# Two PSUM banks as two tiles instead of one, in the attention bursts of a fused attention and feed-forward kernel

## The chip, the cores and the metric

The kernel runs on one core of one Trainium2 chip. The metric is the device time of one execution in microseconds (us), median over runs. A core has TensorE (PE, whose weight loads the profile lists as PEld), VectorE (DVE), ScalarE (ACT), GpSimd (POOL) and SyncE (SP, which issues the DMAs). Each engine runs its own list of instructions in order and waits for other engines through semaphores.

## The reference

Linear attention with decay, in blocks of 64 tokens, then a feed-forward layer with a squared ReLU. All in float32. Per batch (4) and head (8), with sequence 768 and head size 64:

```
for each block of 64 tokens:
    intra = ((q @ k.T) * Dmask) @ v          # Dmask[i,j] = lam**(i-j) for i >= j, else 0
    inter = (q * lam**(i+1)) @ kv_state
    out   = intra + inter
    kv_state = lam**64 * kv_state + (k * lam**(63-j)).T @ v
x = out as 3072 tokens x 512
h = x @ w_in                                  # 512 -> 2048
y = (max(h, 0) ** 2) @ w_out                  # 2048 -> 512
```

## The kernel before, in words

**Units of work.** Tokens go in chunks of 128 (two blocks of 64), numbered t = 0 to 23, six to a batch. Four chunks make a slice m of 512 tokens, the width of one feed-forward step; there are six slices. The 2048 hidden features go in 16 groups f of 128. Float32 products of the feed-forward layer are made of three products of a high and a low part (wh, wl for weights, xh, xl or gh, gl for data).

**Stages.** The opening does the attention of chunks 0 to 3. Then come two plain slices (m = 0 and 1, the constant PLAIN): for each f, `hidden` (L574) makes h by 12 matmuls, ACT and DVE square it and split it into gh and gl (`positive`, `square`, `rest`), and `project` (L605) adds the product of the group before into four accumulators `acc`. In m = 0 the attention of chunks 4 to 7 is spread over the f loop (`look`, `attend`). In m = 1, the "slice 2" of the change's title, each of f = 0 to 8 holds one **burst** (L430) for chunk t = 8 + f. After that two pairs of slices are done by a seven-product scheme (`pair`, L760, 8 calls to a pair of slices); in the first pair of slices each call holds a burst for chunks 17 to 24, the last of which has no chunk ahead.

**A burst** is attention work of TensorE alone, in matmuls of 64 by 64 by 64 that run on the four quarters of the array, all recorded at line 384. Its three parts, in the order of the code:

- `scores(t)`: k by q of chunk t, 16 matmuls (each is two records in the trace, 32 in all). Those with operands on partitions 0 to 63 (row 0) write the half `hi_` of bank y (a tile named h from the pool ps_h), those on partitions 64 to 127 (row 1) the half `lo_` of bank x[1].
- `result(t - 1)`: masked scores by v, and q by the state, of the chunk before: 32 matmuls (64 records); row 0 writes the other half of y, row 1 the half `lo_` of x[0].
- `news(t)`: k by v of chunk t, which feeds the state: up to 16 matmuls (32 records); row 1 writes the half `hi_` of x[0], row 0 the half `hi_` of x[1].

x[0] and x[1] are the two banks of one tile `att` from the pool ps_a, which holds one such tile at a time. So bank x[1] is written first by row 1 (scores) and later by row 0 (news). Between the two stands the **mark**: a copy of one element on ACT (L439) that reads the last score in x[1]. It stands on ACT behind what the argument `meanwhile` issues: in slice 2 that is `positive(h)` (L588), in a pair it is `positive(c21)` and `square_high(c21)`. Nothing reads the marked value; the copy is there for the waits it makes.

**What sets the order.** Each engine's order is the order of the code. The framework puts in the waits: an instruction that writes a tile waits for earlier readers and writers of that tile on other engines. The first matmul of `result` that writes att waits for the mark, since both touch att.

**After a burst** ACT copies the result out of y and x[0] (`keep`, L447), DVE reads the scores (`masked`, L463, two reads) and the news (`state`, L483, first from x[0], then from x[1]), POOL scales q of the next chunk (`prep_q`, L452) and k (`prep_k`), ACT makes copies with the partition halves swapped (`copy_vx` L162, `copy_qx` L167), and SP issues loads for later chunks (`load_v` L151, `load_kq` L145 and L132). In f = 2, 3, 4, 6, 7 and 8 (and later in 10 and 12) of slice 2, `w_parts` (L662) also writes sums of weights to memory, which the pairs fetch again.

**PSUM** has eight banks: ps_h two, ps_a two (one `att` tile), and four for ps_o in the opening, which are given back and taken by the accumulators ps_acc.

Of the kernel before, what the change touches and what calls it, by code (L numbers as in the profile page):

```python
# [7 lines left out]
F32 = mybir.dt.float32  # L8
# [5 lines left out]
PSUM = bass.MemoryType.PSUM  # L14

P = 128
# [6 lines left out]
DM = H * D  # L23
# [19 lines left out]
def body(ctx: ExitStack, tc: tile.TileContext, qT, kT, kvq, lam, w, out):  # L43
# [3 lines left out]
    wk = ctx.enter_context(tc.tile_pool(name="wk", bufs=2))  # L47
    small = ctx.enter_context(tc.tile_pool(name="small", bufs=1))
    ps_h = ctx.enter_context(tc.tile_pool(name="ps_h", bufs=2, space=PSUM))
    ps_a = ctx.enter_context(tc.tile_pool(name="ps_a", bufs=1, space=PSUM))  # L50
    opening = ExitStack()
    ps_o = opening.enter_context(tc.tile_pool(name="ps_o", bufs=2, space=PSUM))
    V = nc.vector
    rows = [slice(j * D, (j + 1) * D) for j in range(2)]
# [18 lines left out]
    def two_banks(pool, name):  # L73
        return pool.tile([P, 2, DM], F32, name=name)
# [62 lines left out]
    def load(t):  # L137
        place(t)
        load_all(t)
        load_kf(t)  # L140
# [9 lines left out]
    def load_v(t):  # L150
        nc.sync.dma_start(out=chunk[t]["v_flat"], in_=kvq[t, :, DM : 2 * DM])  # L151

    def load_vx(t):
        for y, r in enumerate(rows):
            nc.sync.dma_start(
                out=chunk[t]["vx"][r].rearrange("p a j d -> p (a j d)"),
                in_=kvq[t, rows[1 - y], DM + 2 * y * C : DM + 2 * (y + 1) * C],
            )
# [115 lines left out]
    x = ZP  # L274
# [12 lines left out]
    for k in range(4):  # L287
# [10 lines left out]
        lambda o, x, y, op=op: V.tensor_tensor(out=o, in0=x, in1=y, op=op)  # L298
# [4 lines left out]
    lo_, hi_ = s[:, 0 : NS - 1], s[:, 1:NS]  # L303
# [16 lines left out]
    for k in range(NS - 1):  # L320
        n = 1 << k
        x = (tr if k else s)[:, k : k + 1]
# [67 lines left out]
    def of(x):  # L390
        return [x[:, k] for k in range(2)]

    def scores(t, banks, begun=(), keys=range(2)):
        g = Group(banks, begun, keys)
        sc_of[t] = [x[:, 0 : NPR * L] for x in banks]
        k_, q_ = chunk[t]["kf"], chunk[t]["q"]
        for b in range(2):
            for a in range(2):
                for y in range(2):
                    for j, r in enumerate(rows):  # L400
                        p = 2 * y + a
                        g.put(
                            j, y, (2 * b + a) * L,
                            k_[r, p, (1 - b) * L : (2 - b) * L], q_[r, p, b * L : (b + 1) * L],
                        )
        return g.begun

    def news(t, banks, at, begun=(), keys=range(2)):
        g = Group(banks, begun, keys)
        k_, v_ = chunk[t]["k"], chunk[t]["v"]  # L410
        n = 2 if t % NCB < NCB - 1 else 1
        u_of[t] = [banks[1 - b][:, at : at + NPR * D] for b in range(n)]
        for a in range(2):
            for j in range(2):
                for y in range(2):
                    for b in range(n):
                        r, p = rows[1 - b], 2 * y + a
                        g.put(1 - b, y, at + (2 * a + j) * D, k_[r, p, j], v_[r, p, j])
        return g.begun
# [8 lines left out]


    def burst(t, done, ahead, meanwhile):  # L430
        x = of(two_banks(ps_a, "att"))
        y = ps_h.tile([P, DM], F32, name="h")
        lo_, hi_ = slice(0, NPR * L), slice(NPR * L, DM)
        begun = set()
        if ahead:
            begun = scores(t, [y[:, hi_], x[1][:, lo_]], begun, "ec")
        meanwhile()
        if ahead:
            nc.scalar.copy(mark[:, 2:3], sc_of[t][1][D : D + 1, NPR * L - 1 : NPR * L])  # L439
        o = [y[:, lo_], x[0][:, lo_]]  # L440
        if done:
            begun = result(t - 1, o, begun, "ea")
        if ahead:
            news(t, [x[1][:, hi_], x[0][:, hi_]], 0, begun, "ca")
        return o

    def keep(t, o):  # L447
# [126 lines left out]
    def hidden(m, f, xh, xl):  # L574
        h = ps_h.tile([P, N], F32, name="h")
        for _ in range({1: 10, 2: 6}.get(f, 0) if m == 0 else 0):
            nc.tensor.matmul(h, wh[:, 0, 0:P], xh[:, 0], start=True, stop=True)
        k = 0
        for wt, x in ((wh, xh), (wl, xh), (wh, xl)):
            for kt in range(KT):  # L580
                nc.tensor.matmul(  # L581
                    h, wt[:, w_in(f), kt * P : (kt + 1) * P], x[:, kt], start=k == 0, stop=k == 11
                )
                k += 1
        return h

    def positive(h):
        nc.scalar.activation(h, h, AF.Relu)  # L588
# [207 lines left out]
    def new_x(m):  # L796
        xs_of[m] = [wk.tile([P, KT, N], F32R, name=n, tag=n) for n in ("xh", "xl")]
# [96 lines left out]
    for m in range(PLAIN):  # L894
        if m == 0:
            new_x(1)
        else:
            held += [
                wk.tile([P, KT, N], F32, name=f"held{k}", tag=n) for k, n in enumerate(("xh", "xl"))
            ]  # L900
        for f in range(NF):
            h = hidden(m, f, *xs_of[m])
            if m == 0:
                t = G + f // 4
                step = f % 4
                u_ = f + 2
                if step == 2:
                    o = two_banks(ps_a, "att")
                    result(t, of(o))
                    if t + 1 < 2 * G:  # L910
                        load(t + 1)
                        load_vx(t + 1)
                    else:
                        for n in (t + 1, t + 2):
                            load_kq(n)
                            load_v(n)
                if step == 1:
                    masked(t)
                    advance(t, 0)
                if u_ < NLOT:  # L920
                    if f:
                        clamp(u_)
                    if f == 1:
                        upper(u_ - 1)
                        lower(u_ - 1)
                    if f:
                        shift(u_)
                    sign(u_)
                if f > 1:
                    upper(u_ - 1)  # L930
                    lower(u_ - 1)
                if f:
                    turn(u_ - 1)
                if step == 1:
                    fade(t, 1)
                    advance(t, 1)
                if f == 0:
                    positive(h)
                    gh = square(h)
                    rest(m, f, h, gh)  # L940
                if u_ < NLOT:
                    rounded(u_)
                    wload(u_ + 3)
                if step == 0 and f:
                    prep_q(t)
                if step == 3 and t + 1 < 2 * G:
                    prep_k(t + 1)
                if f:
                    positive(h)
                    gh = square(h)  # L950
                    rest(m, f, h, gh)
                if step == 1:
                    copy_qx(t)
                if step == 2:
                    attend(t, o)
                if u_ + 1 < NLOT:
                    first(u_ + 1)
                if prev is not None:
                    project(*prev)
                if step == 0:  # L960
                    look(t)
                    fade(t, 0)
            else:
                t = 2 * G + f
                if f == 0:
                    prep_k(t)
                if f <= 2 * G:
                    x = burst(t, f > 0, True, lambda: positive(h))
                    rest(m, f, h, square(h))
                else:  # L970
                    squared(m, f, h)
                if 1 <= f <= 2 * G:
                    keep(t - 1, x)
                if f <= 2 * G:
                    masked(t)
                    state(t)
                    if f:
                        load_v(t + 1)
                    prep_q(t)
                    if t + 2 < SOLO:  # L980
                        load_kq(t + 2)
                    prep_k(t + 1)
                    copy_vx(t)
                if f - 1 in SUMS:
                    w_parts(SUMS.index(f - 1), S)
                if f in SUMS:
                    S = w_sums(SUMS.index(f))
                if f <= 2 * G:
                    copy_qx(t)
                if f == 2 * G + 1:  # L990
                    fetch(0)
                    fetch(1)
                if f > 2 * G:
                    x_sums(f - 2 * G - 1)
                    x_parts(f - 2 * G - 1)
                project(*prev)
            prev = (m, f)
# [6 lines left out]
    for d in range((NM - PLAIN) // 2):  # L1004
        m1, m2 = PLAIN + 2 * d, PLAIN + 2 * d + 1
        last = d == (NM - PLAIN) // 2 - 1
        for i in range(NPAIR):
            t = (PLAIN + 2) * G + i
# [93 lines left out]
```

## Time and profile before

| | |
|---|---|
| median of 3 runs | 596.24 us (596.09 to 596.43) |
| profiled execution | 595.19 us; its span, first to last instruction, 593.4 us, so 1.79 us lie around it |
| mean granted clock of TensorE | 0.997 |
| busy: PE, PEld | 578.0 us (97%), 471.8 us (80%) |
| busy: DVE, ACT, POOL | 320.4 us (54%), 316.7 us (53%), 70.9 us (12%) |
| chain that ended last | PE 88%, DVE 5%, ACT 5%, issue 1%, DMA 1% |
| DMA | 93.62 MB, mean 158 GB/s |

Times in the views are microseconds from the start of the span. A PE record is a matmul with a modelled end: matmuls overlap, so what counts as time on PE is the distance between starts, and the idle time that a view names before a record is shorter than the hole between the starts. In the timeline, equal instructions close together are merged into one row with their count, and a bracket gives the idle time before the row and what ended it.

### The profile page before, as it was taken

The page shows a single profiled execution, that of the slowest core. Times are in us where ns is not written, and L with a number is a line of the kernel's source. Part 1 is how long each engine was busy: PE and PEld are TensorE (multiplying, and loading weights), DVE is VectorE, ACT ScalarE, POOL GpSimd, SP SyncE. Part 2 cuts the span into 40 slices and gives each one's busy share as a digit, 9 for nine tenths or more (in the row PEclk, how much of TensorE's full clock was granted, in tenths as well). Part 3 has the DMA queues.
Part 4 walks back from the last instruction along what each step waited for, and adds up shares of the span by engine and source line. Part 5 has one row for each costly group of instructions (what it writes and reads, how often), then busy time and mean ns, then how long its engine had stood idle before and what let it go on. Part 6 is the DMA issues. An engine that isn't in the chain of part 4 may idle for free.

```text
span 593.4 us, 12762 instructions
## 1 busy us (share of the span) xinstructions
PE 578.0 (97%) x5240; PEld 471.8 (80%) x5240; DVE 320.4 (54%) x586; ACT 316.7 (53%) x579; POOL 70.9 (12%) x87
## 2 busy tenths in 40 slices
PE   8799999999999999999999999999999999999997
PEld 5677788787787888888888788888888888888885
DVE  7889999946867676534443333356433333334222
ACT  4598888945666555455454455543444444444221
POOL 7302221221323100011101010000000000000000
PEclk9999999999999999999999999999999999999999
DMA  8658567146897942855555554300264444421001
GB/s 333 223 203 276 176 233 264 38 144 196 276 363 234 357 151 98 273 172 180 161 143 159 176 163 118 132 1 0 58 192 125 122 124 120 122 62 72 1 0 71
DMA packets 51273, 93.62 MB, mean 158 GB/s; under 512 B 4624, under 2 KB 19472, under 8 KB 51216
## 3 DMA queue, kind: packets, MB, share of 16 engines
q1 hardware_dynamic: 51216, 92.82, 48.5%
q8 instruction: 41, 0.67, 0.5%
q14 instruction: 16, 0.13, 0.1%
HBM read 71.83 MB, written 20.97 MB: 156 GB/s over the span
## 4 chain that ended last, share of the span: by engine, by line
PE 88%; DVE 5%; ACT 5%; issue 1%; DMA 1%; POOL 0%; ACTq 0%; DVEq 0%; POOLq 0%
PE h L723 24%; PE acc L617 15%; PE acc L622 14%; PE acc L618 14%; PE h L581 12%; PE att L384 5%; PE h L384 2%; PE att L79 1%; DVE temp L298 1%; DVE A L232 1%; ACT gh L592 1%; ACT temp L588 1%; DMA raw<-in_w 1%; PE open L384 1%; DVE A L238 1%
## 5 line engine op out<-in xcount | busy, mean ns | idle before, releaser
L617 PE MATMUL acc<-wh,gh 128*128 128x512 f32 x384 | 151.9, 396 | 0.0
L618 PE MATMUL acc<-wl,gh 128*128 128x512 f32 x384 | 149.5, 389 | 0.0
L622 PE MATMUL acc<-wh,gl 128*128 128x512 f32 x384 | 149.4, 390 | 0.0
L617 PEld LDWEIGHTS acc<-wh,gh 128*128 128x128 f32 x384 | 72.0, 188 | 15.6
L622 PEld LDWEIGHTS acc<-wh,gl 128*128 128x128 f32 x384 | 72.1, 188 | 15.4
L618 PEld LDWEIGHTS acc<-wl,gh 128*128 128x128 f32 x384 | 72.1, 188 | 14.5
L602 DVE TENSOR_TENSOR gl<-h,gh 128x512 fp32r<-128x512 f32 x48 | 33.1, 689 | 74.2 <-ACT h L597 74.2
L588 ACT ACTIVATE h<-h 128x512 f32<-128x512 f32 x48 | 27.9, 582 | 74.0 <-PE h L581 40.3
L298 DVE TENSOR_TENSOR temp<-h,temp 128x512 f32<-128x512 f32 x48 | 33.0, 688 | 60.5 <-PE h L723 49.4
L723 PE MATMUL h<-wh,ring 128*128 128x512 f32 x224 | 60.0, 390 | 0.0
L588 ACT ACTIVATE temp<-temp 128x512 f32<-128x512 f32 x16 | 10.1, 632 | 88.6 <-DVE temp L298 88.6
L723 PEld LDWEIGHTS h<-wh,ring 128*128 128x128 f32 x224 | 42.0, 188 | 8.9 <-DVE r L298 0.3
L456 POOL TENSOR_TENSOR qs<-set,qpow 128x512 f32<-128x512 f32 (+1 forms) x21 | 24.9, 1187 | 179.2 <-PE att L384 160.9
L581 PE MATMUL h<-xh,wl 128*128 128x512 f32 x128 | 34.9, 394 | 1.6 <-DVE wl L247 1.5
L581 PE MATMUL h<-xh,wh 128*128 128x512 f32 x128 | 34.8, 394 | 1.1 <-ACT xh L562 0.7
L298 DVE TENSOR_TENSOR r<-h,temp 128x512 f32<-128x512 f32 x24 | 16.6, 692 | 34.1 <-PE h L723 33.0
L723 PE MATMUL h<-wl,ring 128*128 128x512 f32 x112 | 34.5, 389 | 0.0
L602 DVE TENSOR_TENSOR gl<-r,gh 128x512 fp32r<-128x512 f32 x24 | 16.6, 690 | 32.9 <-ACT gh L755 32.9
L581 PE MATMUL h<-xl,wh 128*128 128x512 f32 x128 | 34.2, 389 | 0.0
L755 ACT CAST gh<-r 128x512 fp32r<-128x512 f32 x24 | 14.9, 621 | 30.0 <-PE acc L618 30.0
L581 PEld LDWEIGHTS h<-xh,wl 128*128 128x128 f32 x128 | 23.6, 188 | 8.5 <-DVE wl L247 3.7
L723 PE MATMUL h<-wh 128*128 128x512 f32 x112 | 30.1, 390 | 0.0
(165 smaller groups left out, 1026.0 us busy)
## 6 DMA issues: line engine op xcount, KB each, us to landing
ring<-wd SPq DMA_DIRECT2D x56, 256.0 KB, 2.8
raw<-in_w SPq DMA_DIRECT2D x22, 512.0 KB, 5.5
set<-in_kvq SPq DMA_DIRECT2D x16, 512.0 KB, 4.2
wd<-hl SPq DMA_DIRECT2D x16, 512.0 KB, 5.8
wh<-wd SPq DMA_DIRECT2D x28, 256.0 KB, 2.8
wl<-wd SPq DMA_DIRECT2D x28, 256.0 KB, 2.9
set<-in_kT SPq DMA_DIRECT2D x22, 256.0 KB, 4.7
set<-in_w SPq DMA_DIRECT2D x10, 512.0 KB, 5.0
```

The source lines that it names most:

```text
L79: nc.tensor.matmul(w_[:, 0], st[:, 0, 0].rearrange("p a b -> p (a b)"), st[:, 0:2].rearrange("p n c a b -> p (n c a b)"), start=True, stop ...
L298: lambda o, x, y, op=op: V.tensor_tensor(out=o, in0=x, in1=y, op=op)
L384: nc.tensor.matmul(self.banks[row][rows[col], at : at + D], lhsT, rhs, start=key not in self.begun, stop=stop, skip_group_check=True,)
L456: nc.gpsimd.tensor_tensor(out=z, in0=x, in1=w_, op=ALU.mult)
L581: nc.tensor.matmul(h, wt[:, w_in(f), kt * P : (kt + 1) * P], x[:, kt], start=k == 0, stop=k == 11)
L588: nc.scalar.activation(h, h, AF.Relu)
L602: V.tensor_tensor(out=gl, in0=r, in1=gh.bitcast(F32), op=ALU.subtract)
L617: nc.tensor.matmul(accs[m][i], gh[:, cs], wh[:, j], start=f == 0, stop=False)
L618: nc.tensor.matmul(accs[m][i], gh[:, cs], wl[:, j], start=False, stop=False)
L622: nc.tensor.matmul(accs[m][i], gl[:, cs], wh[:, j], start=False, stop=end)
L723: nc.tensor.matmul(bank, w[:, kw * HALF + kt * P : kw * HALF + (kt + 1) * P], x_slot(2 * c + kt, kx), start=first and q == 0, stop=q == 5, ...
L755: nc.scalar.copy(gh, r_of[f])
```

## The change

`burst` takes two one-bank tiles b0 and b1 from a new pool ps_b in place of one two-bank tile. The pool ps_a, now placed at the right end of PSUM, is given back before m = 1, and ps_b is opened in its place. The first burst (f = 0 of m = 1), which has no result to make, no longer issues the mark, and its news of row 0 go to the half `lo_` of bank y, where row 0 has written its scores, instead of x[1]. Everything else of the kernel is as before.

```diff
     ps_h = ctx.enter_context(tc.tile_pool(name="ps_h", bufs=2, space=PSUM))
-    ps_a = ctx.enter_context(tc.tile_pool(name="ps_a", bufs=1, space=PSUM))
-    opening = ExitStack()
+    opening, middle = ExitStack(), ExitStack()
+    ps_a = middle.enter_context(tc.tile_pool(name="ps_a", bufs=1, side="right", space=PSUM))
     ps_o = opening.enter_context(tc.tile_pool(name="ps_o", bufs=2, space=PSUM))
...
     def burst(t, done, ahead, meanwhile):
-        x = of(two_banks(ps_a, "att"))
+        x = [ps_b.tile([P, DM], F32, name=f"b{k}") for k in range(2)]
         y = ps_h.tile([P, DM], F32, name="h")
         lo_, hi_ = slice(0, NPR * L), slice(NPR * L, DM)
         begun = set()
         if ahead:
             begun = scores(t, [y[:, hi_], x[1][:, lo_]], begun, "ec")
         meanwhile()
-        if ahead:
+        if ahead and done:
             nc.scalar.copy(mark[:, 2:3], sc_of[t][1][D : D + 1, NPR * L - 1 : NPR * L])
         o = [y[:, lo_], x[0][:, lo_]]
         if done:
             begun = result(t - 1, o, begun, "ea")
         if ahead:
-            news(t, [x[1][:, hi_], x[0][:, hi_]], 0, begun, "ca")
+            news(t, [x[1][:, hi_] if done else y[:, lo_], x[0][:, hi_]], 0, begun, "ca" if done else "ea")
         return o
...
         if m == 0:
             new_x(1)
         else:
+            middle.close()
+            ps_b = ctx.enter_context(tc.tile_pool(name="ps_b", bufs=1, side="right", space=PSUM))
             held += [
```

The order of the instructions stays as it was on every engine, apart from the one mark that goes. What moves is where waits stand. On TensorE, in the burst of a pair (the third of them; h_3509 or h_3524 is bank y, att_3508 the two-bank tile, b0_3522 and b1_3523 the two new tiles), the result begins like this before:

```order
L384 MATMUL att_3508<-set0_92 64x64
L384 MATMUL h_3509<-a_3052,set0_92 64x64 x2
L384 MATMUL att_3508<-a_3052,vx_95 64x64 [waits Activation_49]
L384 MATMUL att_3508<-a_3052,vx_95 64x64
L384 MATMUL h_3509<-a_3052,set0_92 64x64 x2
L384 MATMUL att_3508<-a_3052,vx_95 64x64 x2
```

and like this now:

```order
L384 MATMUL b1_3523<-set0_92 64x64
L384 MATMUL h_3524<-a_3064,set0_92 64x64 x2
L384 MATMUL b0_3522<-a_3064,vx_95 64x64 x2
L384 MATMUL h_3524<-a_3064,set0_92 64x64 x2
L384 MATMUL b0_3522<-a_3064,vx_95 64x64 x2
L384 MATMUL h_3524<-a_3064,vx_95 64x64 x2
```

The wait for ACT before the second pair of result matmuls is gone there. In slice 2 a wait for ACT stays at that place, since those matmuls read vx, which ACT copied in the f before; the mark it can't be, because the mark reads b1 and no matmul of the result touches b1. At the end of the same burst of the pair, on TensorE, where the news begin, before:

```order
L384 MATMUL att_3508<-qx_91,st_83 64x64
L384 MATMUL att_3508<-qs_94,st_83 64x64
L384 MATMUL att_3508<-v_3051,set0_92 64x64 [waits DMAHW2_49,Pool_49]
L384 MATMUL att_3508<-v_3051,set0_92 64x64 x15
L617 MATMUL acc_3232<-wh_97,gh_3465 128x512
```

and now:

```order
L384 MATMUL b0_3522<-qx_91,st_83 64x64
L384 MATMUL b0_3522<-qs_94,st_83 64x64
L384 MATMUL b0_3522<-v_3063,set0_92 64x64 [waits DMAHW2_49,Pool_49]
L384 MATMUL b1_3523<-v_3063,set0_92 64x64 [waits Activation_49]
L384 MATMUL b0_3522<-v_3063,set0_92 64x64
L384 MATMUL b1_3523<-v_3063,set0_92 64x64
```

The wait for ACT's mark now stands at the first matmul of the news that writes b1, 32 result matmuls later. In the first burst of slice 2, on TensorE, between the last score and the news, before:

```order
L384 MATMUL h_1644<-set0_92 64x64
L384 MATMUL att_1643<-set0_92 64x64
L384 MATMUL att_1643<-set0_92 64x64 [waits DMAHW3_49,Activation_49,Pool_49]
L384 MATMUL att_1643<-set0_92 64x64 x15
L617 MATMUL acc_732<-wh_97,gh_1610 128x512
```

and now:

```order
L384 MATMUL h_1649<-set0_92 64x64
L384 MATMUL b1_1648<-set0_92 64x64
L384 MATMUL b0_1647<-set0_92 64x64 [waits DMAHW3_49,Pool_49]
L384 MATMUL h_1649<-set0_92 64x64
L384 MATMUL b0_1647<-set0_92 64x64
L384 MATMUL h_1649<-set0_92 64x64
```

The wait for ACT is gone; the news alternate between b0 and bank y.

## Rows read from the trace of the kernel before

**Rows 1.** The page, busy time of the engines (share of the span, instructions).

```profile
PE 578.0 (97%) x5240; PEld 471.8 (80%) x5240; DVE 320.4 (54%) x586; ACT 316.7 (53%) x579; POOL 70.9 (12%) x87
```

**Rows 2.** The page, the chain that ended last, by engine.

```profile
PE 88%; DVE 5%; ACT 5%; issue 1%; DMA 1%; POOL 0%; ACTq 0%; DVEq 0%; POOLq 0%
```

**Rows 3.** Waits of PE: us in total, times, longest us.

```profile
PE att L384 <- ACT mark L439: 3.1, 15, 0.2
```

**Rows 4.** The instructions of line 439: ns min/median/max, first and last start.

```profile
L439 ACT COPY mark<-att x16: 152/152/152, 131.7 to 358.7; 1x1 f32<-1x1 f32 x16
```

**Rows 5.** Timeline of PE, a burst of slice 2: start, us, operation.

```profile
154.74 0.27 PE L384 MATMUL h<-set 64*64 64x64 f32 x1
...
155.25 0.29 PE L384 MATMUL h<-a,set 64*64 64x64 f32 x4
155.76 0.27 PE L384 MATMUL att<-a,vx 64*64 64x64 f32 x2 [0.22 <-ACT mark L439]
...
156.69 0.22 PE L384 MATMUL att<-qs,st 64*64 64x64 f32 x1
...
157.31 0.50 PE L617 MATMUL acc<-wh,gh 128*128 128x512 f32 x1
```

**Rows 6.** Timeline of ACT, the same burst.

```profile
151.94 0.41 ACT L167 COPY qx<-qs 64x256 f32<-64x256 f32 x1
154.85 0.58 ACT L588 ACTIVATE h<-h 128x512 f32<-128x512 f32 x1 [2.50 <-PE h L581]
155.56 0.15 ACT L439 COPY mark<-att 1x1 f32<-1x1 f32 x1
```

**Rows 7.** Timeline of PE, first and last slice 2 burst with a result.

```profile
138.75 0.29 PE L384 MATMUL h<-a,set 64*64 64x64 f32 x4
139.25 0.27 PE L384 MATMUL att<-a,vx 64*64 64x64 f32 x2 [0.22 <-ACT mark L439]
...
196.29 0.29 PE L384 MATMUL h<-a,set 64*64 64x64 f32 x4
196.79 0.27 PE L384 MATMUL att<-a,vx 64*64 64x64 f32 x2 [0.22 <-ACT mark L439]
```

**Rows 8.** Timeline of PE, first and last burst of a pair with a mark.

```profile
252.30 0.29 PE L384 MATMUL h<-a,set 64*64 64x64 f32 x4
252.78 0.27 PE L384 MATMUL att<-a,vx 64*64 64x64 f32 x2 [0.19 <-ACT mark L439]
...
358.47 0.29 PE L384 MATMUL h<-a,set 64*64 64x64 f32 x4
358.95 0.27 PE L384 MATMUL att<-a,vx 64*64 64x64 f32 x2 [0.19 <-ACT mark L439]
```

**Rows 9.** Timeline of PE, the first burst: last score, then the news.

```profile
131.38 0.22 PE L384 MATMUL att<-set 64*64 64x64 f32 x1
131.95 0.69 PE L384 MATMUL att<-set 64*64 64x64 f32 x32 [0.34 <-issue]
```

**Rows 10.** Timeline of PE, the last burst, which has a result and no mark.

```profile
375.70 0.27 PE L384 MATMUL h<-a,v 64*64 64x64 f32 x2
375.71 0.27 PE L384 MATMUL att<-a,vx 64*64 64x64 f32 x2
...
376.64 0.22 PE L384 MATMUL att<-qs,st 64*64 64x64 f32 x1
```

**Rows 11.** Timeline of DVE (slice 2) and of ACT (a pair): idle time left.

```profile
156.85 0.69 DVE L602 TENSOR_TENSOR gl<-h,gh 128x512 fp32r<-128x512 f32 x1 [1.30 <-ACT h L597]
...
294.00 0.59 ACT L766 COPY temp<-h 128x512 f32<-128x512 f32 x1 [0.40 <-PE h L723]
```

**Rows 12.** DMA in slice 2: a stretch (windows), an issue (timeline), landing (line 151).

```profile
155.00:172.00 17.00, 16.57 (x324) 13.55 (x313) 10.52 (x25) 10.69 (x23) 4.07 (x4) 1.00 1.06 358
...
164.74 0.34 SPq L151 DMA_DIRECT2D set<-in_kvq  x1
...
DMA to landing us min/median/max: 3.2/4.8/6.0
```

## The prediction

> **What bounds the kernel now.** I read the page's busy times first: PE is busy 97% of the span, the next engine apart from PE's own weight loads is DVE with 54% [rows 1]. Then the chain that ended last: 88% of it is PE, and DVE and ACT hold 5% each [rows 2], so PE sets the time and a change pays where PE stands still. The waits of PE name the place: matmuls on att wait 15 times for ACT's mark, 3.1 us in all [rows 3]. That sum is too small a measure, because matmuls in flight count as busy. The timeline shows the true hole. In a burst of slice 2 [rows 5] the scores start at 154.74, the first result matmuls (bank y) follow at 155.25, and the next one in PE's order, which writes att, starts only at 155.76. ACT shows why [rows 6]: it works on `positive` from 154.85, for 0.58 us, and only then does the mark, 155.56 plus 0.15, which ends 0.05 us before PE goes on. PE stands for 0.51 us per burst, in order, with 29 result matmuls behind the blocked one, the news, and the whole of `project`.
>
> **What an unblocked result looks like.** The last burst has a result and no mark [rows 10]: bank y starts at 375.70, att at 375.71, and the last att record starts at 376.64. So the two streams run side by side, 0.01 us apart, and a stream of 16 steps takes 0.93 us from first to last start, 0.058 us a step. In the blocked burst att takes the same 0.93 us (155.76 to 156.69, [rows 5]) once it is let go. The wait is thus not hidden in the result: it moves its end one for one.
>
> **The change, part by part.**
>
> *Two tiles for two banks.* The mark reads b1; the result writes y and b0 alone. So the result's wait for the mark goes, in every burst that has both. There are 16 marks [rows 4]; 15 stand before a result, 8 in slice 2 and 7 in the pairs.
> - Slice 2: the hole is 139.25 - 138.75 = 0.50 us in the first and 196.79 - 196.29 = 0.50 in the last [rows 7], 0.51 in the one above. Less the 0.01 that att trails y anyway: 0.49 each, 8 x 0.49 = 3.92 us.
> - Pairs: 252.78 - 252.30 = 0.48 and 358.95 - 358.47 = 0.48 [rows 8], so 7 x 0.47 = 3.29 us.
>
> *Where the wait goes.* The news into b1 now wait for the mark. With the result starting at 155.26 and 0.93 + 0.06 us long, the news come up at about 156.25; the mark is seen by PE at 155.76. It is hidden with 0.49 us to spare, in the pairs 0.5 likewise (result from 252.30 to about 253.29, mark seen at 252.78). If that cover went (an ACT that is late by more than 0.5 us), the news would wait for the difference.
>
> *Waits that appear.* In slice 2 the mark also covered three waits for older work of ACT, which now stand on their own: vx (at the place of the old wait) and twice qx. The copies were done long before: the last qx copy of that f started at 151.94 and took 0.41 [rows 6], 2.9 us ahead of the result. So three waits are new in a burst of slice 2 (two for qx, one at the news) and one in a pair. A wait that is met costs an issue at most, between nothing and one step of 0.06 us: (8 x 3 + 7) x 0.06 = 1.9 us as the upper end. I take nothing, since the result of rows 5 holds a met wait for POOL in its middle and keeps the pace of rows 10.
>
> *The first burst.* The mark and the wait of the news for it go, because row 0 writes its news to the bank of its own scores. The last score started at 131.38, the next step would be 131.44, the news came at 131.95 [rows 9]: 0.51 us. ACT loses one copy of 0.15 us there, beside PE, worth nothing. The state update reads bank y instead of the other bank, the same size. The new place of the pools costs nothing: in rows 5 matmuls into two pools' banks run at one pace.
>
> **Sum.** 3.92 + 3.29 + 0.51 = 7.72 us less on PE.
>
> *What is late next.* Where PE comes 0.5 us sooner, the others must keep up. In slice 2 a step of f is (196.29 - 138.75) / 7 = 8.22 us [rows 7]; DVE, at its fullest f, idles 1.30 us before gl [rows 11] and ACT 2.50 us before `positive` [rows 6], both more than 0.5. In a pair ACT has 0.40 us left before it copies the next pair's first product [rows 11]; 0.47 takes that up, and the copy comes 0.07 late, but PE does the whole next product (six matmuls) before it needs that bank again. So no new stall there. POOL and SP start their work for the next chunk after the result, so sooner too.
>
> *DMA.* This is the closest thing to a second limit. From 155 to 172 the DMA engines are busy throughout (share 1.06, 358 GB/s), and the loads of v take up to 6.0 us to land [rows 12]. The news of rows 5 begin at 156.75; two steps of f later, at 173.2, come those that use the load issued at 164.74, 8.4 us after it. Issue and news both follow the end of a result, so after the change it is one shorter step, 7.9 us. Three f in a row write weights, each 0.49 us shorter, so the queue grows by up to 1.5 us: 6.0 + 1.5 = 7.5, still under 7.9. I take nothing; the upper end is that DMA sets the pace of six steps of f, which then keep their old length: 6 x 0.49 = 2.9 us of the gain lost.
>
> The profiled execution took 595.19 us (span 593.4 and 1.79 around it), so it would take 587.5. The median of the runs, 596.24, lies 1.05 above it; I subtract the same 7.7 there: **588.5 us**.
>
> **Rivals.**
>
> 1. *PE can't be fed faster.* Scores, result and news become up to 128 records without a stop, and the hole may have served to refill PE's supply of instructions. For it: no row shows a whole burst without a hole. Against it: the result of rows 10 passes without a hole, 64 records in 1.0 us, 16 ns each, and in rows 5 the step after the hole is the same. Priced at half of each hole lost, 15 x 0.25 = 3.75 us: 592.2. In its strong form the supply needs the whole 2.57 us that a burst takes now (154.74 to 157.31, [rows 5]); then the hole is mere slack and the time stays at 596.2. The Trainium skill has a rule that would do this: TensorEngine Tiling (Array Packing), Performance Considerations, Instruction Overhead, gives each matmul about 60 cycles of overhead, from which I estimate 25 ns at 2.4 GHz and 3.2 us for 128. The 16 ns of rows 10 speak against it.
>
> 2. *DMA keeps six steps of f at their length*: 588.5 + 2.9 = 591.4. For it the full queue, against it the 7.9 us of room, where a landing takes 6.0 [rows 12].
>
> 3. *The wait doesn't go.* The wait for ACT that stays at the result in slice 2 holds PE as the mark did, because ACT's count passes it only later. Then slice 2 gains in the first burst alone: 596.2 - 3.3 - 0.5 = 592.4; if the pairs kept a wait too, 595.7. Against it: vx is copied in the f before, 2.9 us earlier at the latest.
>
> 4. *Slower: v comes late.* Shorter steps in a full DMA queue push the landing of v past the news, and PE stands there with `project` behind it. The point from which it costs is a landing of 7.9 us. Six f write weights; at 10 us (6.0 is the most now) each of their bursts waits 2.1 us, 12.6 us in all, against the 7.7 gained: 601.1. It turns slower from a landing of 9.2 us. For it only the share of 1.06; against it that the queue grows by 1.5 us at most.
>
> **How the numbers follow.** My forecast 0.82; rival 1 0.07 (0.05 at half a hole, 0.02 in its strong form); rival 2 0.05; rival 3 0.04 (half with the pairs free, half without); rival 4 0.02. A measurement here tells 0.2%, 1.2 us, from no change. Faster by more than that: 0.82 + 0.05 + 0.05 + 0.02 = 0.94. Within: 0.02 + 0.02 = 0.04. Slower: 0.02. The range: the low end is the profiled execution with all 16 holes gone whole, 595.19 - 8.0 = 587.2; the high end takes in the waits that appear (590.4) and rival 2, 588.5 + 2.9 = 591.4, and leaves out rivals 1, 3 and 4, 0.13 together.
>
> **What would show it.** In the changed kernel's timeline the record that writes b0 starts 0.01 us behind the first result record of y; a burst lasts 2.57 - 0.49 = 2.08 us from first score to `project`; the waits of PE for the mark are gone or under 0.3 us in all. I am wrong if a hole of 0.3 us or more stands at the first b1 record of the news, if the step inside a burst stretches beyond 0.058 us, or if PE waits for a load of v.

## The result and the profile after

The changed kernel takes **587.1 us** (median of 5 runs, 586.2 to 587.43), the kernel before, run beside it on the same chip, 596.43 (596.09 to 596.73): a ratio of 0.984, 95% interval 0.9826 to 0.9855, or 9.3 us less. I had forecast 588.5, with 587.2 to 591.4 as the range. The direction and the mechanism held; the gain was larger than the 7.7 us of the sum, and the time lies 0.1 us below the range.

The page after, busy times and chain:

```profile
PE 574.1 (98%) x5240; PEld 469.8 (80%) x5240; DVE 318.7 (55%) x586; ACT 315.2 (54%) x578; POOL 73.2 (13%) x87
...
PE 91%; DVE 4%; ACT 3%; issue 1%; DMA 1%; POOL 0%; DVEq 0%; ACTq 0%; POOLq 0%
```

The span fell from 593.4 to 584.6 us, the profiled execution from 595.19 to 586.32. PE's share of the chain rose from 88% to 91%, ACT's fell from 5% to 3% [rows 2]. The waits of PE, longest in total first:

```profile
PE h L384 <- DVE st L490: 1.4, 3, 0.5
PE att L79 <- POOL st L70: 1.3, 1, 1.3
```

The mark, which led this list with 3.1 us in 15 waits [rows 3], is gone from it. The timeline of PE shows a burst of slice 2, the one that answers to [rows 5]:

```profile
152.62 0.27 PE L384 MATMUL h<-set 64*64 64x64 f32 x1
...
153.13 0.22 PE L384 MATMUL h<-a,set 64*64 64x64 f32 x1
153.14 0.22 PE L384 MATMUL b<-a,vx 64*64 64x64 f32 x1
...
153.20 0.22 PE L384 MATMUL b<-a,vx 64*64 64x64 f32 x1
...
153.26 0.22 PE L384 MATMUL b<-a,vx 64*64 64x64 f32 x1
...
154.07 0.64 PE L384 MATMUL b<-set 64*64 64x64 f32 x16
154.64 0.50 PE L617 MATMUL acc<-wh,gh 128*128 128x512 f32 x1
```

The result's two streams start 0.01 us apart, as forecast, and go on at 0.06 us a step. From first score to `project` the burst takes 154.64 - 152.62 = 2.02 us; before it took 157.31 - 154.74 = 2.57 [rows 5]. On ACT the mark still stands behind `positive`, and nobody waits for it:

```profile
152.72 0.58 ACT L588 ACTIVATE h<-h 128x512 f32<-128x512 f32 x1 [2.37 <-PE h L581]
153.44 0.15 ACT L439 COPY mark<-b 1x1 f32<-1x1 f32 x1
```

**Where the time went.** I took the starts of all matmul records and added up the 17 bursts, each from its first score to the first record of `project`: 40.61 us before, 32.20 after, so 8.40 less. What lies between and behind the bursts is 417.48 us in both. The opening, from PE's first matmul to the first burst, took 129.59 and 129.15 us. It varies from run to run: in the runs below with the same opening code, one profiled execution each, it took 128.06 to 130.87. So the bursts are the right measure, good to some 0.01 us each but for one that is told of below, and medians carry about a microsecond of the opening.

### The profile page after: what moved, and what is told of

It reads as the page before. It is cut to its first block, busy times and chain, and to the rows that moved or that the text cites. A ratio compares the mean times of both kernels' runs of the same rounds, so it can differ in the third digit from the quotient of the medians.

```text
span 584.6 us, 12762 instructions
## 1 busy us (share of the span) xinstructions
PE 574.1 (98%) x5240; PEld 469.8 (80%) x5240; DVE 318.7 (55%) x586; ACT 315.2 (54%) x578; POOL 73.2 (13%) x87
## 4 chain that ended last, share of the span: by engine, by line
PE 91%; DVE 4%; ACT 3%; issue 1%; DMA 1%; POOL 0%; DVEq 0%; ACTq 0%; POOLq 0%
PE h L723 26%; PE acc L617 15%; PE acc L622 14%; PE acc L618 14%; PE h L581 12%; PE h L384 4%; PE b L384 2%; PE att L79 1%; PE att L384 1%; DVE A L232 1%; PE open L384 1%; DVE A L238 1%; ACT A L208 1%; DMA raw<-in_w 1%; ACT faded L508 0%
## 5 line engine op out<-in xcount | busy, mean ns | idle before, releaser
L456 POOL TENSOR_TENSOR qs<-set,qpow 128x512 f32<-128x512 f32 (+1 forms) x21 | 27.0, 1284 | 167.9 <-PE b L384 156.8
```

The source lines that it names most:

```text
L456: nc.gpsimd.tensor_tensor(out=z, in0=x, in1=w_, op=ALU.mult)
```

## The experiments

Theory: the gain is the hole at the mark, whole, and the wait moved to the news is covered. Rivals: a part of the gain comes from the first burst's own edit or from the place of the pools; the wait at the news is covered only just, or not at all; PE can't be fed through a burst without a hole.

**The change again, and its parts.** e0_again is the changed kernel. e1_first_only is the kernel before with the first burst's edit alone (no mark without a result, its news in y). e2_tiles_only is the change without that edit. e3_place_only keeps the one tile of two banks and moves the pools as the change does:

```diff
-        x = of(two_banks(ps_a, "att"))
+        x = of(two_banks(ps_b, "att"))
...
+            middle.close()
+            ps_b = ctx.enter_context(tc.tile_pool(name="ps_b", bufs=1, side="right", space=PSUM))
```

> The changed kernel once more, on the chip of the next three. My theory now: each hole on TensorE cost its length and a restart of about 0.05 us, so 15 x 0.53 + 0.55 = 8.5 us are the change's own, and the rest of the 9.3 us between the medians is scatter of the opening; here 1.2 to 1.7% below before, 587.0 to 588.0 us. Rival (the place of the pools in PSUM helps the opening): again 9.3 us or more below before.

> The kernel before with the edit of the first burst alone (its news of row 0 in bank y, no mark; one two-bank tile in all bursts). My theory: one hole of 0.51 us and its restart of 0.05 go, 0.55 us below before. Rival (the first burst is worth more than its hole, since POOL, DVE and the accumulators of the slice before hang on it): 1 us or more below.

> The changed kernel with the old first burst (mark, news in b1), two tiles everywhere. My theory: 15 holes with their restarts go, 7.9 us below before, 0.55 us above the changed kernel. By the terms of the prediction (no restart) 7.2 us below before.

> The kernel before with the change's pools and their place in PSUM (ps_a at the right end, given back before the second slice, ps_b in its place), but ps_b holds one two-bank tile as before and the first burst is the old one. My theory: as before within 0.3 us. Rival (place helps): 0.4 to 0.9 us below before.

| run | median us | ratio to before (595.57), 95% | bursts, sum us |
|---|---|---|---|
| e0_again | 586.6 | 0.9855 (0.9836 to 0.9873) | 32.09 |
| e1_first_only | 594.67 | 0.9983 (0.997 to 0.9996) | 39.97 |
| e2_tiles_only | 586.62 | 0.9851 (0.9834 to 0.9869) | 32.98 |
| e3_place_only | 594.99 | 0.9994 (0.9983 to 1.0005) | 40.60 |

e0_again lies 1.45% below before, as expected, and its median just under the 587.0 to 588.0 that I had put. In the bursts the place of the pools is worth nothing (40.60 against 40.61). The rival was an opening that gains 0.4 to 0.9 us by it, and e3's ratio alone (0.4 us less, between 1.0 less and 0.3 more) doesn't rule that out. But take from each run's fall in median the fall of its bursts: 0.6 us is left in e3 and 0.5 in e0, and as much, 0.3 and 0.7, in e1 and e6 (below), which keep the old place. So what is left doesn't go with the place. The first burst's edit alone is worth 0.57 us in its own burst (1.665 to 1.092). In e2 that burst stays at 1.61 us, because its news wait for the mark at their first record on b1:

```profile
129.86 0.32 PE L384 MATMUL b<-set 64*64 64x64 f32 x3
130.38 0.69 PE L384 MATMUL b<-set 64*64 64x64 f32 x30 [0.19 <-ACT mark L439]
```

With no result between scores and news there is nothing that hides the moved wait. The median of e2 doesn't show this 0.5 us; in its profiled execution the opening was the shortest of all (128.06 us). A further 0.37 of its sum is one later burst, told of below. All the rest of the gain in the bursts is the two tiles'.

**The pairs alone given back.** e7_pairs_one is the change with one tile of two banks again for the bursts of the pairs:

```diff
-        x = [ps_b.tile([P, DM], F32, name=f"b{k}") for k in range(2)]
+        x = [ps_b.tile([P, DM], F32, name=f"b{k}") for k in range(2)] if t <= 4 * G else of(two_banks(ps_c, "att"))
```

> The changed kernel with one two-bank tile again in the bursts of the pairs, two tiles in slice 2 alone. Theory (the parts add up): the seven bursts of the pairs with a mark go back from 2.03 to 2.54 us, 3.6 us above the changed kernel, slice 2 stays at 2.03. Rival (pairs gain little, ACT has only 0.40 us of room there): under 2 us above.

590.96 us, ratio 0.9927 (0.9907 to 0.9948). The pairs' bursts are back at 2.54 us, those of slice 2 stay at 2.025 but for the one told of below; the sum is 35.80, 3.6 above the change. The wait is back seven times:

```profile
PE att L384 <- ACT mark L439: 1.3, 7, 0.2
```

The parts add: 3.6 us for the pairs, 4.3 for slice 2 (8 x 0.542), 0.57 for the first burst.

**What makes the hole.** e6_mark_first is the kernel before with the mark ahead of `positive` in slice 2. My prediction read the hole as ACT's work on `positive`.

```diff
-        meanwhile()
+        first = t <= 4 * G
+        if not first:
+            meanwhile()
         if ahead:
             nc.scalar.copy(mark[:, 2:3], sc_of[t][1][D : D + 1, NPR * L - 1 : NPR * L])
+        if first:
+            meanwhile()
```

> The kernel before with the mark ahead of positive on ACT in the nine bursts of slice 2. The prediction's reading (ACT works on positive and only then on the mark): the hole all but goes there, bursts of 2.57 us fall to 2.1, 4 us below before. Rival, my theory now (the hole is the way from PE's last score to ACT and back, since the last score ends no sooner than positive): bursts stay at 2.5 to 2.57 us, the time within 0.5 us of before.

594.86 us against 596.04, ratio 0.9982 (0.997 to 0.9994). By the prediction's reading 4 us should have gone; about 1 did, more than the 0.5 I had allowed, and only 0.44 of it stands in the bursts (40.17 us). ACT, idle for 2.97 us, takes the mark as soon as it may, and PE still stands:

```profile
154.97 0.15 ACT L441 COPY mark<-att 1x1 f32<-1x1 f32 x1 [2.97 <-PE att L384]
155.14 0.58 ACT L592 ACTIVATE h<-h 128x512 f32<-128x512 f32 x1
```

```profile
154.68 0.22 PE L384 MATMUL att<-set 64*64 64x64 f32 x1
...
154.72 0.29 PE L384 MATMUL h<-a,set 64*64 64x64 f32 x4
155.17 0.27 PE L384 MATMUL att<-a,vx 64*64 64x64 f32 x2 [0.16 <-ACT mark L441]
...
155.28 0.23 PE L384 MATMUL att<-a,vx 64*64 64x64 f32 x2
...
155.34 0.22 PE L384 MATMUL att<-a,vx 64*64 64x64 f32 x2
```

The hole is 155.17 - 154.72 = 0.45 us instead of 0.51, the burst 2.511 instead of 2.567. So 0.45 us is the way from PE's last score over an idle ACT back to PE, and `positive` added 0.06. The rows give its parts: the last score runs from 154.68 to 154.90 (a modelled end), the mark from 154.97 to 155.12, and PE goes on at 155.17. These rows also hold the term that I missed: after the hole the next att record comes 0.11 us later (155.17 to 155.28), and only then does the step fall to 0.06. In the changed kernel's rows above it is 0.06 from the start of the result.

**How much cover the moved wait has.** e4_late_2 and e5_late_6 delay the mark in the changed kernel by two and by six copies of one element:

```diff
+            for k in range(6):
+                nc.scalar.copy(mark[:, 4 + k : 5 + k], fd[0:1, 0:1])
             nc.scalar.copy(mark[:, 2:3], sc_of[t][1][D : D + 1, NPR * L - 1 : NPR * L])
```

> The changed kernel with two more one-element copies on ACT ahead of each of the 15 marks, some 0.17 us each, so that the mark comes 0.34 us later. Theory (the wait now stands at the news, with about 0.5 us to spare): still hidden, bursts of 128 records stay at 2.03 us, the time of the changed kernel within 0.3 us. Rival (the moved wait is not covered): each of 12 bursts that write news to b1 grows by 0.34 us, 4 us in all.

> The same with six copies, the mark 1.0 us later, past the 0.5 us of cover. Theory: a hole of about 0.5 us at the news of b1, and with the restart of 0.05 to 0.1 us behind it a burst of 2.55 to 2.65 us in the 12 bursts that write news to b1; the three without (112 records by missing news: chunks 11, 17, 23) stay at 2.03. In all 6.2 to 7.4 us above the changed kernel. Without a cost of the restart it would be the hole alone, 0.5 us, 6 us.

e4 gave 588.01 us (0.9868, 0.9848 to 0.9888; before is 596.04 here) with bursts of 128 records at 2.025, no hole. Its median is 1.4 above 586.6, not within the 0.3 expected; its profiled execution, 587.99, has the longest opening (130.87 us) and 0.25 in one burst that is told of below. e5 gave 589.68 (0.9901, 0.9881 to 0.9921); its bursts sum to 34.42, 2.3 more than in e0_again, where I had expected 6.2 to 7.4: a miss. ACT's rows of a burst whose first score is at 145.93:

```profile
146.03 0.58 ACT L590 ACTIVATE h<-h 128x512 f32<-128x512 f32 x1 [3.06 <-PE h L583]
146.64 0.66 ACT L440 COPY mark<-fd 1x1 f32<-1x1 f32 x6
147.32 0.15 ACT L441 COPY mark<-b 1x1 f32<-1x1 f32 x1
```

Six copies in a row take 0.66 us, not six times the 0.15 of one, so the delay was smaller than I had reckoned. The mark starts 1.39 us after the first score, in the changed kernel 153.44 - 152.62 = 0.82: 0.57 later. This burst and four more of slice 2 grow by 0.191 us: 0.14 of hole at the news, and 0.05 that comes with the hole. So the cover is 0.57 - 0.14 = 0.43 us, where I had worked out 0.49. The first with a result grows by 0.06, most of the pairs' by 0.13. Two bursts, of chunks 13 and 19, grow by 0.42 and 0.36: their result is 0.23 us shorter (the burst takes 1.79 us in the change), so only some 0.2 us covers the mark there. In e4, whose mark comes 0.20 us later, the first of these two is the only one that the delay lengthens, by 0.05. Bursts whose chunk makes no news on b1 (t = 11, 17 and 23) stay at their length, which shows that the hole is this wait.

**The supply of instructions.** In some runs of the changed kernel one burst, that of f = 6 in slice 2, is longer: 2.136 us in the changed kernel's first trace, 2.396 in e2, 2.278 in e4, 2.121 in e7, but 2.025 in e0. The extra lies at about records 114 to 118 of its 128. The three kernels below shift the program by small matmuls behind `warm(4)`, 57 of them in the change (e8_shift_57), 57 in the kernel before (e9_before_57), 28 in the change (e10_shift_28); nothing reads their output.

```diff
     warm(4)
+    tiny = two_banks(ps_a, "att")
+    for _ in range(57):
+        nc.tensor.matmul(tiny[0:D, 0, 0:8], st[0:D, 0, 0, 0], st[0:D, 0, 0, 1, 0:8], start=True, stop=True)
```

> The changed kernel with 57 small matmuls of 64x8 (114 records) behind the first four of the opening; nothing reads what they write. The burst of f = 6 in slice 2 takes 2.14 us in the changed kernel's trace, 2.40 in e2_tiles_only, 2.28 in e4_late_2, and 2.03 in e0_again; the extra lies at record 114 to 118 of its 128, in the issue, and no semaphore ends it. Theory A (supply of instructions): the trace shows 41 packets of 16 KB in the instruction queue for 5240 matmul records, one to 128 records; the record where PE stands is the first of a new packet, and it stands because 114 quick records of the burst are through before the packet is there. With 114 records more ahead of it the edge of a packet falls on the burst's start, so that a whole packet is spent in the 2.0 us of the burst: no stand at record 114, but one at its end, of 0.3 to 3 us, seen as a later start of project or of its second record (burst up to project's second record 2.3 to 5 us, against 2.2 now). The median then lies 0.3 to 3 us above 586.6, less or more the opening's cost of the small matmuls, up to 2 us. Theory B (something that belongs to that place of the program, such as the load of v or a wait that no row names): the stand stays at record 114 to 118 of the same burst, up to 0.4 us, wherever the packets' edges lie; time 586.6 plus the opening's cost.

> The kernel before with the same 57 small matmuls. Its burst of f = 6 lasts 2.57 us with the hole at the mark. Theory A: the hole gives the packet 0.5 us more to come, so that the stand at the end of the burst is 0.5 us shorter than in e8_shift_57, from nothing to 2.5 us. Theory B: no stand at the end, burst 2.57, time that of the kernel before plus the opening's cost of 0 to 2 us.

> The changed kernel with 28 small matmuls (56 records). The edge of a packet then falls in the middle of the burst of f = 6, some 58 records into it, and the packet before holds 70 records of slower work (hidden and project at 0.23 us a record, so over 10 us). Theory A: no stand in this burst, 2.03 us; other bursts, where an edge lies after 90 or more burst records, may show one. Theory B: the stand stays at record 114 to 118 of the burst of f = 6, 0.1 to 0.4 us. Time 586.6 in both, plus the opening's cost of 0 to 1 us.

Medians 598.03, 607.33 and 591.64 us against 595.41; ratios 1.0049 (1.0032 to 1.0066), 1.0192 (1.0168 to 1.0216) and 0.9946 (0.993 to 0.9963). They are far above what I had allowed for, and say little here: the small matmuls alone take 7.4 us in e8's timeline and 4.0 in e10's, and the opening took 139.2, 141.5 and 137.7 us. The clock is part of that: over the first 50 us of the span TensorE's mean granted clock was 0.83, 0.80 and 0.76 in the three, where it was 0.97 in the kernel before and 0.93 in the changed one. The bursts answer the question. In f = 6 the stand is gone with either shift (2.025 us in e8 and e10), so it doesn't belong to that place of the program: theory B falls. The stand that theory A expected at the end of that burst in e8 didn't come, a miss. But new ones came in bursts that never had one: in the pairs' bursts the second one is 2.654 us and the fourth 2.251 in e10, the fifth 2.548 in e8, where each of these takes 2.025 in the change. The timeline of PE in e10 (the second), then in e8:

```profile
273.56 0.28 PE L387 MATMUL b<-set 64*64 64x64 f32 x4
274.16 0.68 PE L387 MATMUL b<-set 64*64 64x64 f32 x28 [0.31 <-issue]
```

```profile
326.47 0.30 PE L387 MATMUL b<-v,set 64*64 64x64 f32 x7
327.02 0.62 PE L387 MATMUL b<-v,set 64*64 64x64 f32 x25 [0.26 <-issue]
```

Nothing that the trace lists released them ("issue"). Counted from 0 among all matmul records of a run, PE stood ahead of record 2379 in f = 6 of e2 and e4; e10's two stands lie at 3264 and 3639, e8's at 3891: 7, 10 and 12 steps of 126 further on, to within 3 records. 126 and not 128 is what a packet would hold if PE's other instructions in the list (branches, semaphores) take the rest. And ahead of each stand one packet of the instruction queue moved, in e10 within this stretch of the DMA view (start 271.87, end 272.83):

```profile
q8 instruction: 1, 0.02, 6.0%
```

PE goes on 1.2 to 1.5 us after that packet's end: e10 274.16 - 272.83 = 1.33 and, at its other stand, 1.38; e8 327.02 - 325.60 = 1.42; e2 176.91 - 175.45 = 1.46; e4 179.13 - 177.81 = 1.32; the changed kernel's first trace 1.21. Where the packet had ended earlier, as in e0 2.8 us before PE came to that record, PE didn't stand. In e9, whose hole at the mark gives 0.5 us, the burst that stood in e8 takes only 0.013 more than the pairs' usual 2.540 instead of 0.523; another of its bursts, the third of the pairs, is 0.12 longer. So the stand goes with the packets, not with the code.

Why a packet comes late stays open. In the changed kernel it started at 175.05, when PE was at record 2263, in e0 at 173.59 and record 2256: 0.42 and 2.02 us before the burst's first score. A full DMA while it moves isn't the reason. The data queue's share of the DMA engines around the packet was 31% in the changed kernel, where PE stood, and 99% in e0, where it didn't (windows 175.0 to 176.05 and 173.5 to 174.6):

```profile
q1 hardware_dynamic: 72, 0.12, 31.1%
q8 instruction: 1, 0.02, 5.7%
```

```profile
q1 hardware_dynamic: 212, 0.39, 99.4%
q8 instruction: 1, 0.02, 5.3%
```

The packet itself took 0.96 us in the first and 0.93 in the second. Ahead of it the engines were full in both; but in e10 they had been idle from 268.0 to 269.8 us, 2 us before the packet of its first stand, so that a queue of data doesn't explain every late packet either.

## Why the prediction was right, and where it was wrong

**Right: the place and the way of the gain.** The wait for the mark went from every result, the b0 record starts 0.01 us behind y's, full bursts last 2.02 us (2.08 forecast), PE's wait for the mark is gone, and no hole stands at the news. The pools' place is worth nothing in the bursts (e3). Met waits cost nothing: bursts outside the hole keep their pace, and all that lies between bursts keeps its 417.48 us. So 0 was right, and the upper end of 1.9 was not needed.

**The moved wait is hidden**, with 0.43 us of cover (e5) where the prediction had 0.49, and some 0.2 in the two bursts with a shorter result. e2's first burst shows the cost without cover, 0.52 us.

**DMA** kept up. From 152 to 167 us, the stretch that answers to [rows 12]:

```profile
152.00:167.00 15.00, 15.00 (x288) 12.43 (x287) 11.54 (x28) 9.91 (x22) 4.06 (x4) 1.00 1.07 377
```

The share is 1.07 where it was 1.06, at 377 GB/s where it was 358, and the loads of v take at most 5.8 us where I had put 7.5. PE waits for none. Rivals 2 and 4 fell. Rival 3 fell with PE's list of waits, which no longer has the mark.

**Rival 1** fell as a general rule: 128 records pass in 2.025 us, 16 ns each, in all but a burst or two. The 60 cycles a matmul of the Trainium skill, TensorEngine Tiling (Array Packing), Performance Considerations, would by the prediction's estimate have made 3.2 us of it; the 16 ns decide against it for four streams side by side. But its mechanism exists: one burst of the changed kernel loses 0.11 us to the supply of instructions, and up to 0.63 is seen in e10. I had priced it at 15 bursts, and it strikes one.

**Wrong: the size of the hole.** The step that failed is the sum, "3.92 + 3.29 + 0.51 = 7.72 us less on PE", whose terms are 8 x 0.49, 7 x 0.47 and the first burst's 0.51. It rests on the reading that a blocked result, once let go, takes no longer than an unblocked one. The whole difference per burst was 0.542 in slice 2, 0.516 in the pairs and 0.573 in the first, together 8 x 0.542 + 7 x 0.516 + 0.573 = 8.5 us. The 0.05 us per burst that is missing is the restart: when PE goes on after a stand, the first four records are followed by a step of 0.087 us in place of 0.038. It is in the kernel before, in the burst of [rows 5]:

```profile
155.76 0.27 PE L384 MATMUL att<-a,vx 64*64 64x64 f32 x2 [0.22 <-ACT mark L439]
...
155.87 0.23 PE L384 MATMUL att<-a,vx 64*64 64x64 f32 x2
...
155.93 0.23 PE L384 MATMUL att<-a,vx 64*64 64x64 f32 x2
```

0.11 us, then 0.06. The prediction found nothing of it, because I compared with the last burst [rows 10], whose result stands at a start of its own and so holds a restart too: 0.93 us from first to last att start in both. The reference for "unblocked" had the cost inside, and it cancelled. Against the score stream that runs on into the result there is none. With 8.5 the same working gives 596.24 - 8.5 = 587.7, which lies inside the range. So the restart is 0.8 of the 1.4 us between 588.5 and 587.1. The other 0.6 is not the bursts' (32.20 and 32.09 in two runs of the change, 8.4 and 8.5 less than before); it is within what the opening varies by, and its cause stays open.

**Wrong: the low end of the range.** It took 16 whole holes, 8.0 us, off the profiled execution as if that were the most that could go. The holes were the least, since each brings its restart: with 8.5 the low end would have been 595.19 - 8.5 = 586.7, below the measured 587.1. And nothing was left for the microsecond by which the opening varies.

**Wrong: the reason given for the hole.** "ACT shows why [rows 6]: it works on `positive`" took a coincidence of two ends for a cause. In the burst of [rows 5] and [rows 6] `positive` ends at 154.85 + 0.58 = 155.43, and the last score, which the mark has to wait for in any case, at 155.22 + 0.22 = 155.44:

```profile
155.22 0.22 PE L384 MATMUL att<-set 64*64 64x64 f32 x1
```

e6 takes `positive` out of the way, and 0.45 of the 0.51 us stays: the round trip between two engines alone. The forecast didn't suffer, since the change removes the wait whatever fills it.

## What to carry to other kernels

A wait of one engine for a one-element instruction on another costs the round trip, some 0.45 us here, however idle the other is; moving that instruction ahead of 0.58 us of work bought 0.06 a burst, moving the wait behind the result's independent 0.9 us bought all of it. Two banks of one tile wait as one: where readers and writers touch different banks, two tiles let the order show. When a hole is measured, measure to where the stream is back at its pace, against a stretch that ran through without a start.

## What the runs showed of the hardware that I had not expected

- **A stand of PE costs a restart** of some 0.05 us: behind the first four records the step is 0.087 us instead of 0.038, at every burst's start and after the mark's hole at every result, in all traces. In the first burst's hole and at e10's stands it is spread over other steps (58 and 35 ns in place of 38 and 7) and comes to the same 0.05.
- **Instructions can be late for a stream of small matmuls.** The instruction queue moves 41 packets, 0.67 MB, in a run: 16 KB each, and 5240 / 41 makes some 128 matmul records (each with its weight load) to a packet. 128 quick records are through in 2.0 us, and where PE stood it went on 2.2 to 2.4 us after its packet had started to move: stands of 0.10 to 0.63 us, in a burst or two of a run, at the packets' edges. The Trainium skill, Runtime: NRT & Kernel Launch, Instruction fetch mechanics, has the blocks of 16 KiB and 256 instructions, which the count agrees with, and calls the crossing mostly hidden; at 16 ns a record it is not always.
- **A small matmul takes a whole step of its stream.** e8's 57 matmuls of 64x8, 114 records in a row on one quarter, go 58 ns apart: the same 58 ns that one stream takes a step inside a burst, at 64 columns. The bursts' 16 ns a record come from four streams side by side. At 11.6 us the granted clock fell from 1.00 (2.4 GHz) to 0.50 (1.2 GHz), though PE had gone on without a pause since its first matmul at 1.32, and the same records went 107 ns apart. The stretches of e8 on either side show the clock (1.00 and 0.50, third number from the end):

```profile
7.00:11.00 4.00, 4.00 (x72) 4.00 (x71) 2.71 (x6) 0.00 (x0) 1.06 (x2) 1.00 1.04 424
12.00:14.00 2.00, 2.00 (x21) 2.00 (x21) 0.00 (x0) 0.00 (x0) 0.00 (x0) 0.50 1.06 437
```
